# ScalarE reads MoE1's relu input from PSUM twice; VectorE subtracts in SBUF

## The chip, the cores and the metric

The kernel runs on one core of a Trainium2 chip. The core has five engines with a queue each: TensorE (PE; PEld is its weight load), VectorE (DVE), ScalarE (ACT), GpSimd (POOL) and SyncE (SP), which only issues DMAs here. Each queue is worked off in order, and engines wait for one another by semaphores. The metric is the time of one execution in microseconds on the device, the median of several runs.

## The reference

Three stages follow one another: chunked attention, a mixture of four experts with relu (MoE1), and a feed-forward layer with a clipped gate (MoE2). All results are fp32; the two weights of the last stage come as 64-bit floats.

```python
scores = scale * q_c @ k_c^T            # chunks of 64 rows, 4 x 8 heads x 576 x 64
attn   = softmax(scores);  x = attn @ v_c          # x: 2304 tokens x 512

p = domain_probs / (domain_probs.sum(-1) + 1e-9)   # MoE1: 4 experts, F = 1024
for e in range(4):
    h = np.maximum(x @ w1[e], 0.0)
    out += p[:, e:e+1] * (h @ w2[e])

h = x @ w_in                                       # MoE2: 512 -> 2048 -> 512
g = h * np.clip(h + 3.0, 0.0, 6.0) / 6.0
return g @ w_out
```

## The kernel before, in words

The large products run in `float32r`. To keep precision, each operand is held as two parts, a high part (the value cast to `float32r`) and a low part (the value minus its high part), and each product is three matmuls: high x high, high x low, low x high (`HL`).

The 2304 tokens are cut into six blocks of 256 or 512 (`sizes`), and two blocks make a set. For each of the three sets the kernel goes through 12 groups of 512 hidden columns, 8 of MoE1 and then 4 of MoE2, and in each group through the blocks of the set. One group of one block is four h slots and four y slots. An h slot (`h_slot`, matmuls L424) computes 128 hidden columns, transposed, into a PSUM bank `psH`; there are two such banks. A y slot (`y_slot`, matmuls L479) multiplies one of the four hidden tiles `gts[f]` with the second weight, into up to four banks `psY` that collect over the four y slots.

Between them stands the relu. In MoE1 ScalarE writes the high part of `gt` from `psH` (L445), and VectorE writes the low part (L446), reading `psH` once more and the high part from SBUF. In MoE2 the gate needs ScalarE's L454 and L461 and VectorE's L458 and L462; L462 is a subtraction whose two inputs both lie in SBUF. The finished `psY` are added into `acc` by VectorE (L503, L507).

The order of the work is written out by hand: each slot issues its matmuls, then the low parts that the slot before left (`late`), then the pieces that a planner assigned to this slot (`early`, `post`) by estimated times. These pieces are the attention of later blocks (`Item`; for instance L315 and L327 on VectorE, L319 on ScalarE, L335 on TensorE), the weights' split into high part (L141, ScalarE) and low part (L142, GpSimd), and in the first set the conversion of the MoE2 weights from 64-bit floats (`Convert`): L163 and L164 on ScalarE, L168, L169, L172, L179 and L183 on VectorE, L184 and L185 on GpSimd. SyncE loads the weights some slots ahead. VectorE adds the finished `psY` of a group in the next group's first two h slots (`TAKE`).

Of the kernel before, what the change touches and what calls it, by code (L numbers as in the profile page):

```python
# [10 lines left out]
F32 = mybir.dt.float32  # L11
F32R = mybir.dt.float32r
U32 = mybir.dt.uint32
AF = mybir.ActivationFunctionType
ALU = mybir.AluOpType
# [10 lines left out]
def raw(ap):  # L26

    return ap.bitcast(F32)
# [3 lines left out]
def fused_kernel(ctx: ExitStack, tc: tile.TileContext, q, k, v, probs, w1, w2, win, wout, out):  # L32
    nc = tc.nc
# [4 lines left out]
    P = 128  # L38
# [22 lines left out]
    sp = pool("sp", 1)  # L61
# [168 lines left out]
    def bank(tag, name="ps"):  # L230
        return pp.tile([P, 512], F32, tag=tag, name=name, bufs=BANKS[tag])
# [139 lines left out]
    late, spread, turns = deque(), deque(), deque()  # L371
# [15 lines left out]
    def slot(pe, now, pre, tail, early, post, take):  # L387


        for fn in pre:  # L390
            fn()
        pe()
        for fn in tail:
            fn()
        old = list(late)
        late.clear()
        for fn in old:
            fn()
        while turns:
            turn(*turns.popleft())  # L400
        for fn in early:
            fn()
        now()
        for _ in range(min(take, len(spread))):
            spread.popleft()()
        for fn in post:
            fn()
# [6 lines left out]
    def h_products(gi, view, f, ds):  # L414

        blk, c0, n = view
        cs = slice(c0, c0 + n)
        w = ws[gi, "h", f].rearrange("p a (d f) -> p a d f", d=KD)
        if (gi, view, f) not in begun:
            begun[gi, view, f] = bank("h", "psH")  # L420
        ps = begun[gi, view, f]
        for d in ds:
            for i, (a, b) in enumerate(HL):
                nc.tensor.matmul(  # L424
                    ps[:, :n], w[:, a, d, :], xt[blk][:, d, b, cs],
                    start=(d == 0 and i == 0), stop=(d == KD - 1 and i == len(HL) - 1),
                )

    def h_slot(gi, view, f, pre, tail, early, post):
        g = gi % NG  # L430
        blk, c0, n = view
        cs = slice(c0, c0 + n)
        done = range(NP // 2) if (gi, view, f) in begun else ()
        if not done:
            begun[gi, view, f] = bank("h", "psH")
        ps = begun[gi, view, f]

        def pe():
            h_products(gi, view, f, [d for d in range(KD) if d not in done])

        gt = sp.tile([P, 2, n], F32R, tag="gt", name="gt", bufs=4, padded_shape=[P, 2, 512])
        gts[f] = gt
        if g < G1:
            def now():
                nc.scalar.activation(gt[:, 0], ps[:, :n], AF.Relu)  # L445
                late.append(lambda: nc.vector.scalar_tensor_tensor(  # L446
                    out=gt[:, 1], in0=ps[:, :n], scalar=0.0, in1=raw(gt[:, 0]), op0=ALU.max, op1=ALU.subtract
                ))
        else:
            u = sp.tile([P, n], F32, tag="u", name="u", bufs=2, padded_shape=[P, 512])  # L450
            r = sp.tile([P, n], F32, tag="r", name="r", bufs=2, padded_shape=[P, 512])

            def now():
                nc.scalar.activation(r, ps[:, :n], AF.Relu, bias=three)  # L454
                late.append(mid)

            def mid():
                nc.vector.scalar_tensor_tensor(  # L458
                    out=u, in0=r, scalar=6.0, in1=ps[:, :n], op0=ALU.min, op1=ALU.mult
                )  # L460
                nc.scalar.mul(gt[:, 0], u, 1.0 / 6.0)  # L461
                late.append(lambda: nc.vector.scalar_tensor_tensor(  # L462
                    out=gt[:, 1], in0=u, scalar=1.0 / 6.0, in1=raw(gt[:, 0]), op0=ALU.mult, op1=ALU.subtract
                ))
        slot(pe, now, pre, tail, early, post, TAKE[f])

    def y_slot(gi, view, f, pre, tail, early, post):
# [283 lines left out]
```

## Time and profile before

| what | value |
|---|---|
| median of three runs | 1308.83 us (1307.6 to 1308.86) |
| the profiled execution, its span | 1307.79 us, 1306.0 us |
| TensorE matmul busy, mean granted clock | 1269.9 us (97%), 0.992 |
| VectorE, ScalarE, GpSimd busy | 601.6, 439.2, 474.7 us |
| L445, relu on ScalarE | 200 instructions, 95.8 us |
| L446, low part on VectorE | 200 instructions, 107.5 us |

A row of the profile names a line, an engine, an operation, what it writes and reads, and how often. "Idle before" is time in which the engine stood still in front of such an instruction, with the one that ended the wait behind the arrow. [...] Busy times are of one profiled execution; they overlap between engines and don't add up to the span.

### The profile page before, as it was taken

To read this page: it belongs to the slowest core of one execution; us is meant where nothing else is said; L and a number is where in the kernel's file an instruction comes from. 1 tells how busy PE (TensorE), PEld (TensorE's weight loads), DVE (VectorE), ACT (ScalarE), POOL (GpSimd) and SP (SyncE) were. 2 spreads that over 40 slices of the span, in tenths; PEclk is the share of its full clock that TensorE was granted. 3 is DMA by queue.
4 is the path that set the end of the run, shared out by engine and by line. 5 is a ranking of instruction groups with operands and counts; after the bars stand their busy time and mean duration, and the time that the engine had idled before them with its cause. 6 is when DMAs were issued, how large, how long until landed. Compare 5 with 4: busy or idle time off the path is not lost.

```text
span 1306.0 us, 19473 instructions
## 1 busy us (share of the span) xinstructions
PE 1269.9 (97%) x7534; PEld 1082.4 (83%) x7534; DVE 601.6 (46%) x990; ACT 439.2 (34%) x880; POOL 474.7 (36%) x359
## 2 busy tenths in 40 slices
PE   8998889889999999999999999999999999999998
PEld 7887777778888888888888888888888888888887
DVE  4547898796355542222233345653222222233443
ACT  4333434333354332222232235433222222234332
POOL 3325677676232233333323233223333333323330
PEclk9999899899999999999999999999999999999999
DMA  7516665553334232222332233423222222222211
GB/s 175 135 63 179 186 189 176 169 162 129 96 91 106 73 97 81 65 65 65 87 83 74 65 101 83 106 68 112 66 63 64 63 65 64 65 59 63 65 33 49
DMA packets 170733, 124.01 MB, mean 95 GB/s; under 512 B 67984, under 2 KB 141712, under 8 KB 170640
## 3 DMA queue, kind: packets, MB, share of 16 engines
q1 hardware_dynamic: 170640, 122.76, 33.0%
q8 instruction: 59, 0.97, 0.3%
q14 instruction: 34, 0.28, 0.1%
HBM read 109.61 MB, written 13.11 MB: 94 GB/s over the span
## 4 chain that ended last, share of the span: by engine, by line
PE 81%; DVE 13%; ACT 2%; DMA 1%; issue 1%; SPq 1%; POOL 1%; DVEq 0%; ACTq 0%; POOLq 0%
PE psH L424 39%; PE psY L479 38%; DVE cm L172 2%; DVE cm L169 2%; DVE cm L168 2%; PE psS L303 1%; DVE ce L179 1%; DVE acc L503 1%; DVE acc L507 1%; DVE gt L446 1%; DVE cm L183 1%; PE psX L346 1%; DVE e L327 1%; PE psT L378 1%; PE psP L335 1%
## 5 line engine op out<-in xcount | busy, mean ns | idle before, releaser
L142 POOL TENSOR_TENSOR ws<-wr,ws 128x512 fp32r<-128x512 f32 x288 | 384.1, 1346 | 758.0 <-ACT ws L141 732.2
L424 PE MATMUL psH<-x,ws 128*128 128x256 f32 (+1 forms) x3552 | 630.7, 335 | 24.6 <-DVE gt L446 23.0
L424 PEld LDWEIGHTS psH<-x,ws 128*128 128x128 f32 x3552 | 545.5, 191 | 99.1 <-DVE gt L446 27.9
L479 PE MATMUL psY<-ws,gt 128*128 128x512 f32 x2592 | 607.2, 391 | 0.0
L479 PEld LDWEIGHTS psY<-ws,gt 128*128 128x128 f32 x2592 | 482.0, 188 | 98.9
L445 ACT ACTIVATE gt<-psH 128x256 fp32r<-128x256 f32 (+1 forms) x200 | 95.8, 479 | 514.2 <-PE psH L424 514.0
L446 DVE SCALAR_TENSOR_TENSOR gt<-psH,gt 128x256 fp32r<-128x256 f32 (+1 forms) x200 | 107.5, 539 | 233.8 <-ACT gt L445 233.8
L141 ACT CAST ws<-wr 128x512 fp32r<-128x512 f32 x288 | 170.3, 615 | 3.8 <-DMA wr<-in_moe_w_dram 2.2
L503 DVE SCALAR_TENSOR_TENSOR acc<-psY,pn,acc 128x512 f32<-128x512 f32 x126 | 89.2, 746 | 168.1 <-PE psY L479 168.1
L454 ACT ACTIVATE r<-psH,three 128x256 f32<-128x256 f32 (+1 forms) x96 | 55.7, 581 | 159.6 <-PE psH L424 158.7
L458 DVE SCALAR_TENSOR_TENSOR u<-r,psH 128x256 f32<-128x256 f32 (+1 forms) x96 | 53.0, 552 | 94.4 <-ACT r L454 94.1
L462 DVE SCALAR_TENSOR_TENSOR gt<-u,gt 128x256 fp32r<-128x256 f32 (+1 forms) x96 | 70.9, 739 | 46.9 <-ACT gt L461 46.8
L461 ACT ACTIVATE gt<-u 128x256 fp32r<-128x256 f32 (+1 forms) x96 | 50.6, 528 | 48.1 <-DVE u L458 48.0
L184 POOL TENSOR_TENSOR w<-w,ce 128x512 f32<-128x512 f32 x32 | 47.7, 1492 | 31.1 <-DVE ce L179 19.6
L507 DVE TENSOR_TENSOR acc<-psY,acc 128x512 f32<-128x512 f32 x54 | 36.0, 687 | 44.8 <-PE psY L479 44.8
L185 POOL TENSOR_TENSOR ce<-w,cm 128x512 f32<-128x512 f32 x32 | 43.6, 1362 | 2.5
L172 DVE SCALAR_TENSOR_TENSOR cm<-w,cm 128x512 uint32<-128x512 uint32 x32 | 35.9, 1123 | 1.1
L169 DVE TENSOR_SCALAR cm<-cm 128x512 uint32<-128x512 uint32 x32 | 35.5, 1110 | 1.1
L168 DVE TENSOR_SCALAR cm<-cm 128x512 f32<-128x512 f32 x32 | 30.1, 940 | 6.2 <-ACT cm L163 6.1
L319 ACT ACTIVATE e<-e 128x512 f32<-128x512 f32 x18 | 11.4, 633 | 52.9 <-DVE e L315 52.9
L363 DVE TENSOR_TENSOR x<-psX,x 128x128 fp32r<-128x128 f32 (+1 forms) x56 | 15.8, 324 | 26.7 <-ACT x L362 25.2
L163 ACT ACTIVATE cm<-w 128x512 f32<-128x512 f32 x32 | 21.5, 673 | 11.6 <-POOL ce L185 11.6
(47 smaller groups left out, 349.9 us busy)
## 6 DMA issues: line engine op xcount, KB each, us to landing
wr<-in_moe_w_dram SPq DMA_DIRECT2D x192, 256.0 KB, 2.8
wr<-win SPq DMA_DIRECT2D x48, 256.0 KB, 2.9
wr<-wout SPq DMA_DIRECT2D x48, 256.0 KB, 2.7
w<-in_moe_w_in_dram SPq DMA_DIRECT2D x16, 512.0 KB, 5.2
w<-in_moe_w_out_dram SPq DMA_DIRECT2D x16, 512.0 KB, 5.2
out_dram<-acc SPq DMA_DIRECT2D x18, 256.0 KB, 2.1
win<-ce SPq DMA_DIRECT2D x16, 256.0 KB, 4.0
wout<-ce SPq DMA_DIRECT2D x16, 256.0 KB, 3.1
```

What stands on the lines that cost most here:

```text
L141: nc.scalar.copy(t[:, 0], self.t)
L142: (eng or nc.gpsimd).tensor_tensor(out=t[:, 1], in0=self.t, in1=raw(t[:, 0]), op=ALU.subtract)
L168: nc.vector.tensor_scalar(out=m, in0=m, scalar1=W_LEAST, scalar2=W_MOST, op0=ALU.max, op1=ALU.min)
L169: nc.vector.tensor_scalar(out=mu, in0=mu, scalar1=4, scalar2=1, op0=ALU.logical_shift_left, op1=ALU.logical_shift_right)
L172: nc.vector.scalar_tensor_tensor(out=mu, in0=self.t[:, :, 1], scalar=0x80000000, in1=mu, op0=ALU.bitwise_and, op1=ALU.bitwise_or)
L424: nc.tensor.matmul(ps[:, :n], w[:, a, d, :], xt[blk][:, d, b, cs], start=(d == 0 and i == 0), stop=(d == KD - 1 and i == len(HL) - 1),)
L445: nc.scalar.activation(gt[:, 0], ps[:, :n], AF.Relu)
L446: late.append(lambda: nc.vector.scalar_tensor_tensor(out=gt[:, 1], in0=ps[:, :n], scalar=0.0, in1=raw(gt[:, 0]), op0=ALU.max, op1=ALU.subtract
L454: nc.scalar.activation(r, ps[:, :n], AF.Relu, bias=three)
L462: late.append(lambda: nc.vector.scalar_tensor_tensor(out=gt[:, 1], in0=u, scalar=1.0 / 6.0, in1=raw(gt[:, 0]), op0=ALU.mult, op1=ALU.subtr ...
L479: nc.tensor.matmul(ps, gt[:, a, j * P:(j + 1) * P], w[:, b, :], start=f == 0 and i == 0, stop=f == GF - 1 and i == len(HL) - 1,)
L503: nc.vector.scalar_tensor_tensor(out=t, in0=ps, scalar=p, in1=t, op0=ALU.mult, op1=ALU.add)
```

## The change

For MoE1 ScalarE reads the bank twice: once into the high part, as before, and once more in full fp32 into a new tile `h32` in SBUF. VectorE then subtracts the high part from `h32`, and no longer reads PSUM for it. The tile takes its place in the buffers of MoE2's tiles `u` (even f) and `r` (odd f), two buffers each. The max with zero, which VectorE computed anew, is now in ScalarE's second relu. Nothing else is changed.

```diff
         if g < G1:
+            h32 = sp.tile([P, n], F32, tag="ur"[f % 2], name="h32", bufs=2, padded_shape=[P, 512])
+
             def now():
                 nc.scalar.activation(gt[:, 0], ps[:, :n], AF.Relu)
-                late.append(lambda: nc.vector.scalar_tensor_tensor(
-                    out=gt[:, 1], in0=ps[:, :n], scalar=0.0, in1=raw(gt[:, 0]), op0=ALU.max, op1=ALU.subtract
+                nc.scalar.activation(h32, ps[:, :n], AF.Relu)
+                late.append(lambda: nc.vector.tensor_tensor(
+                    out=gt[:, 1], in0=h32, in1=raw(gt[:, 0]), op=ALU.subtract
                 ))
```

## Rows read from the trace of the kernel before

**Rows 1.** The page, busy us (share of the span) xinstructions of each engine.

```profile
PE 1269.9 (97%) x7534; PEld 1082.4 (83%) x7534; DVE 601.6 (46%) x990; ACT 439.2 (34%) x880; POOL 474.7 (36%) x359
```

**Rows 2.** Table by stretches: us, busy of each engine, granted clock, DMA share, GB/s.

```profile
99.00:297.00 198.00, 176.62 (x963) 147.82 (x963) 170.48 (x242) 76.26 (x149) 134.48 (x95) 0.95 0.59 180
...
528.00:561.00 33.00, 33.00 (x170) 28.29 (x169) 8.68 (x15) 8.17 (x17) 10.34 (x8) 1.00 0.22 65
```

**Rows 3.** Waits from 99 to 297 us: who for whom, us in total, times, longest.

```profile
PE psH L424 <- DVE gt L446: 21.0, 11, 4.3
...
DVE gt L446 <- ACT gt L445: 13.3, 11, 2.2
ACT cm L163 <- POOL ce L185: 11.6, 5, 3.1
...
DVE cm L168 <- ACT cm L163: 5.7, 10, 1.3
```

**Rows 4.** Timeline of one stall: start us, us, engine line op [idle before].

```profile
231.40 0.41 DVE L446 SCALAR_TENSOR_TENSOR gt<-psH,gt 128x256 fp32r<-128x256 f32 x1
...
231.86 4.61 PE L424 MATMUL psH<-x,ws 128*128 128x256 f32 x24 [1.96 <-DVE gt L446]
...
236.31 5.62 PE L479 MATMUL psY<-ws,gt 128*128 128x512 f32 x24
```

**Rows 5.** Groups by form, 99 to 297 us: count | busy, mean ns | idle before.

```profile
L169 DVE TENSOR_SCALAR cm<-cm 128x512 uint32<-128x512 uint32 x29 | 32.2, 1112 | 1.0
...
L183 DVE TENSOR_SCALAR cm<-cm 128x512 uint32<-128x512 uint32 x29 | 13.4, 461 | 1.0
L446 DVE SCALAR_TENSOR_TENSOR gt<-psH,gt 128x512 fp32r<-128x512 f32 x19 | 12.8, 685 | 7.7 <-ACT gt L445 7.7
...
L446 DVE SCALAR_TENSOR_TENSOR gt<-psH,gt 128x256 fp32r<-128x256 f32 x22 | 9.2, 418 | 5.6 <-ACT gt L445 5.6
```

**Rows 6.** Timeline of VectorE, its idle times in front of L446 and L168.

```profile
101.13 0.42 DVE L446 SCALAR_TENSOR_TENSOR gt<-psH,gt 128x256 fp32r<-128x256 f32 x1 [1.01 <-ACT gt L445]
...
133.09 0.69 DVE L446 SCALAR_TENSOR_TENSOR gt<-psH,gt 128x512 fp32r<-128x512 f32 x1 [1.18 <-ACT gt L445]
134.16 1.07 DVE L168 TENSOR_SCALAR cm<-cm 128x512 f32<-128x512 f32 x1 [0.38 <-ACT cm L163]
...
155.67 0.42 DVE L446 SCALAR_TENSOR_TENSOR gt<-psH,gt 128x256 fp32r<-128x256 f32 x1 [1.85 <-ACT gt L445]
...
260.84 0.81 DVE L168 TENSOR_SCALAR cm<-cm 128x512 f32<-128x512 f32 x1 [0.39 <-ACT cm L163]
...
295.89 0.69 DVE L446 SCALAR_TENSOR_TENSOR gt<-psH,gt 128x512 fp32r<-128x512 f32 x1 [1.25 <-ACT gt L445]
```

**Rows 7.** Timeline of TensorE at the last stall of the stretch.

```profile
290.68 7.22 PE L424 MATMUL psH<-x,ws 128*128 128x512 f32 x24 [3.51 <-DVE gt L446]
297.74 2.43 PE L479 MATMUL psY<-ws,gt 128*128 128x512 f32 x10
```

**Rows 8.** Timeline around 1208 us: MoE2's subtraction in SBUF, beside GpSimd and alone.

```profile
1207.56 1.32 POOL L142 TENSOR_TENSOR ws<-wr,ws 128x512 fp32r<-128x512 f32 x1 [5.64 <-ACT ws L141]
...
1208.05 1.38 DVE L462 SCALAR_TENSOR_TENSOR gt<-u,gt 128x512 fp32r<-128x512 f32 x1 [1.32 <-ACT gt L461]
...
1210.72 0.69 DVE L462 SCALAR_TENSOR_TENSOR gt<-u,gt 128x512 fp32r<-128x512 f32 x1 [0.70 <-ACT gt L461]
```

**Rows 9.** Timeline of VectorE: two steps of a conversion without GpSimd beside them.

```profile
209.56 0.43 DVE L169 TENSOR_SCALAR cm<-cm 128x512 uint32<-128x512 uint32 x1
...
211.21 0.43 DVE L183 TENSOR_SCALAR cm<-cm 128x512 uint32<-128x512 uint32 x1
```

**Rows 10.** Groups by form, whole span: ScalarE's relu.

```profile
L445 ACT ACTIVATE gt<-psH 128x512 fp32r<-128x512 f32 x88 | 52.6, 598 | 255.5 <-PE psH L424 255.5
L445 ACT ACTIVATE gt<-psH 128x256 fp32r<-128x256 f32 x112 | 43.1, 385 | 258.6 <-PE psH L424 258.5
```

**Rows 11.** Waits of TensorE, whole span.

```profile
PE psP L335 <- DVE e L327: 3.6, 4, 1.7
```

## The prediction

> **What bounds the kernel now.** I read the page first, then the waits, the table by stretches, the groups of the one stretch that stood out, and the timeline of its stalls. TensorE is busy 97% of the span [rows 1]: a change to the two vector engines can only win back what TensorE waits for, or make it wait more. Over most of the span there is nothing to win: from 528 to 561 us TensorE works all 33.00 us at clock 1.00, with VectorE at 8.68 [rows 2]. The stretch from 99 to 297 us is different. There the `moe2` weights are converted from 64-bit floats (`Convert`, L163 to L188) beside the first block set, VectorE is busy 170.48 of 198 us, GpSimd 134.48, and TensorE only 176.62 at a granted clock of 0.95. So 198.0 - 176.6 = 21.4 us are lost there, and about 0.05 x 198 = 10 us more to the lower clock.
>
> What TensorE waits for there has one name: L446, 21.0 us in 11 waits [rows 3]. L446 is the second reader of the bank `psH`, and `psH` has two banks. The timeline of one stall shows how it works [rows 4]: the 256-column h slots 0 and 1 run, VectorE is deep in a conversion, L446 for slot 0 comes only at 231.40, slots 2 and 3 start 0.05 us after its end, and the y slots follow when those are done, at 236.31. The chain is conversion -> low part of slot 0 -> two h slots -> y. VectorE is what is late, and TensorE's two h slots are put behind it.
>
> **What the edit takes away.** L446 no longer reads PSUM; both readings are ScalarE's, back to back, so slots 2 and 3 no longer wait for VectorE. But VectorE's subtraction is still in front of something: y slot f reads both halves of `gts[f]` (L479). So the chain becomes conversion -> low part of slot 0 -> y slot 0, with slots 2 and 3 off it. The wait moves three slots further and does not go. As VectorE is busy 86% of the stretch, the length of the stretch after the change is VectorE's work plus what VectorE still idles; I sum it from VectorE's side.
>
> *Idle time of VectorE that goes.* VectorE idles in front of L446 for 7.7 + 5.6 = 13.3 us in the stretch, in 11 waits [rows 5]. Three of about 1.0 us, one of them shown, lie before the first conversion and stay: -3.1. One of 1.2 us ending at 133.09 comes from ScalarE being held by the attention's exponential, and stays. The other 9.0 us, seven waits, are VectorE, having caught up, waiting for h slots that had started late because of it, the first at 155.67 and the last at 295.89 [rows 6]; with TensorE three slots further ahead they go. Of the ten waits of L168 for ScalarE's L163 (5.7 us) [rows 3], five of 0.27 to 0.64 us, at 134.16 the first and at 260.84 the last, stand behind such a late relu and go as well: 2.1 us. Sum 11.1 us; bounds 0 (TensorE never gets ahead) and 19 (13.3 + 5.7, all of it).
>
> *The end of the stretch.* The last stall releases slots 2 and 3 at 290.68 and y starts at 297.74 [rows 7]. After the change y 0 can start where L446 for slot 0 ends, slots 2 and 3 lying before it: 7.1 us once, and not once for each stall, since at the earlier ones VectorE, not TensorE, sets when the next low part comes. Bounds 0 and 7.1.
>
> *What VectorE pays.* The subtraction now has two inputs in SBUF. Undisturbed it costs the same: L462, the operation of that kind here, takes 0.69 us at 512 columns [rows 8], L446 0.69 and 0.42 [rows 5]. Beside a GpSimd operation that also reads SBUF, L462 takes 1.38 us, and ends 0.55 us after GpSimd's does; L446, with one input in PSUM, keeps its 685 and 418 ns means even in this stretch. So 41 operations that were free of GpSimd become exposed to it. Two estimates of the price. First, the conversion's own steps, exposed in the same way: undisturbed L169 takes 0.43 and L183 0.43 us [rows 9], in the stretch 1112 and 461 ns on average [rows 5], the largest and the smallest excess of the five: 0.68 and 0.03 us. The mean of the two, 0.36 us, times 41 is 14.8. Second, chance: GpSimd is busy 134.48 / 198 = 68% with operations of 134.48 / 95 = 1.42 us, so an operation that starts at any time waits 0.68 x 0.71 = 0.48 us; times 41 is 19.7. I take the middle, 17. Bounds: 41 times the excess of L183, 1.3 us, and of L169, 28 us. Not less than zero, since nothing that L446 waits for now goes from this operation.
>
> [...]
>
> *What ScalarE pays.* 200 more readings. A second reading takes at most a whole L445, 598 or 385 ns [rows 10]: 52.6 + 43.1 = 95.7 us, ScalarE from 439 to 535 us of 1306 [rows 1]. It can't be below zero, since nothing of ScalarE's goes. Elsewhere it is hidden: an h slot of 12 matmuls lasts 2.8 us at 512 columns, as 24 take 5.62 us [rows 4], and ScalarE is busy 8.17 of 33 us in the steady stretch [rows 2]. In the conversion stretch it adds at most 19 x 0.598 + 22 x 0.385 = 19.8 us to 76.26 of 198. Queued behind the second reading are the weight casts (L141) and the conversion's first step (L163); GpSimd and VectorE wait for those. VectorE being the later one there, I cost it at nothing; if that cover goes, each of the ten L163 waits is longer by 0.3 to 0.6 us, up to 5 us. A bank also becomes free earlier than by two engines in turn (0.60 + 0.69 against 0.60 + 0.6), which in the steady stretches nobody waits for.
>
> *SBUF and queues.* The new tile lies in the buffers of `u` and `r`, idle in MoE1; it is reused four h slots later, after y slots that need the same subtraction, so no wait is added. No DMA moves.
>
> **Sum.** 11.1 + 7.1 - 17 = 1.2 us gained. The profiled execution took 1307.79 us (span 1306.0 and 1.8 around it), 1.0 us under the median 1308.83 of the runs; it would become 1306.6, and the median 1307.6, which I round to 1307.5. A change under 0.2% (2.6 us) can't be told from none, so this reads as no change. TensorE's 21.0 us on L446 go from the trace, and come back as waits for the low part at L479.
>
> **Rivals.**
> *The collisions are mostly paid already* (faster). The operation behind a subtraction is often a conversion step that waits for the same GpSimd operation anyway: what the one waits, the other no longer does. Then the price falls to about 7 us and the gain is 11.1 + 7.1 - 7 = 11.2: 1297.6. For it: a GpSimd operation can be waited for only once, and there are 95 of them. Against: by the timeline some twelve of the 41 stand in front of an operation that reads PSUM, such as L503, or of a transposition, which pays nothing today.
>
> *VectorE and GpSimd hold each other up at the SBUF* (slower). Place: VectorE between 99 and 297 us. If each subtraction pays what L169 pays, 28 us, the sum is 18.2 - 28 = -9.8: 1318.6. It decides from 18.2 / 41 = 0.44 us per subtraction on, and is seen as slower from (18.2 + 2.6) / 41 = 0.51. For it: conversion steps leave GpSimd with a queue, and the low parts come right behind them; in order on TensorE stand also attention products (L335) that wait for VectorE's L327, 3.6 us in four waits [rows 11], so TensorE can't run ahead everywhere. Against: GpSimd still idles 198.0 - 134.5 = 63.5 us of the stretch.
> [...]
>
> *ScalarE becomes the gate of the banks.* It sits up to 3.1 us behind L163, 11.6 us in five waits for GpSimd's L185 in the stretch [rows 3], and the relu behind it now alone frees the bank. Only what exceeds an h slot (2.8 us, half of it at 256 columns) reaches TensorE: at most some 4 us, 1311.5 where all of it adds to the forecast. Against: L445 sits behind TensorE, not behind L163, in most waits.
>
> **Numbers.** Forecast (within 2.6 us, price between 15.6 and 20.8): 0.38, own range 1306.2 to 1311.4. Faster, price under 15.6: 0.34. Slower: 0.28, of which 0.24 for the collisions and 0.04 for ScalarE. The range runs from a price of 7.5 us (1298) to one of 26.5 (1317).
>
> **What would show it.** Right: no wait of L424 on the low part; waits of L479 on VectorE between 99 and 297 us of about 20 us; the new subtraction at 0.42 and 0.69 us outside the stretch and about 0.4 us longer in it; VectorE's busy time in the stretch up by some 17 us and its idle time in front of the low part nearly gone; nothing after 330 us moved but in time. Wrong: TensorE's lost time in the stretch under 12 us, or the low part there no longer than before (faster); or a stretch longer than 198 us with GpSimd's operations longer too (slower).

## The result, and the profile after

The changed kernel took 1316.96 us (median of 4 runs), the kernel before 1308.21 us beside it: ratio 1.0067, 95% interval 1.0054 to 1.0080, 8.8 us slower. The forecast was no change (1307.5 us); the time lies 0.04 us inside the upper end of the range, far from the forecast and in the part of the range that the prediction gave to its slower rivals. The profiled execution took 1317.56 us, 9.8 us more than the 1307.79 of before. The ratios of all runs leave out one slow execution, of 3236.53 us, among the six of e11.

The page after shows busy time of each engine, and the group of the new subtraction. They answer to [rows 1]: VectorE is busy 33.7 us longer (a third of it outside the conversion; behind 330 us TensorE waits for VectorE 1.9 us, against 2.1 before), ScalarE 73.3 us, TensorE 2.2 us.

```profile
PE 1272.1 (97%) x7534; PEld 1079.8 (82%) x7534; DVE 635.3 (48%) x990; ACT 512.5 (39%) x1080; POOL 482.8 (37%) x359
...
L449 DVE TENSOR_TENSOR gt<-h,gt 128x256 fp32r<-128x256 f32 (+1 forms) x200 | 145.9, 733 | 233.9 <-ACT h L448 233.7
```

The table by stretches of the kernel after (us, busy of each engine, TensorE's granted clock with 1.00 for full speed, DMA share, GB/s) answers to [rows 2]; a row for 297 to 330 us is added.

```profile
99.00:297.00 198.00, 174.73 (x965) 143.19 (x964) 179.91 (x234) 89.50 (x188) 134.73 (x91) 0.96 0.56 170
297.00:330.00 33.00, 27.94 (x141) 22.35 (x139) 32.42 (x35) 14.05 (x29) 25.44 (x17) 1.00 0.49 160
...
528.00:561.00 33.00, 33.00 (x170) 28.33 (x169) 9.01 (x15) 11.22 (x25) 10.33 (x8) 1.00 0.22 64
```

The same view of the kernel before, for the added row:

```profile
297.00:330.00 33.00, 32.56 (x170) 27.69 (x170) 21.73 (x30) 11.39 (x23) 21.43 (x16) 1.00 0.30 98
```

The steady stretch is as it was: TensorE 33.00 of 33.00 us. The conversion stretch lost 23.3 us of TensorE in place of 21.4, and the 33 us behind it 5.1 in place of 0.4. VectorE, at 21.73 us there before, is now busy 32.42 of 33: the conversion is not done by 330 us.

The waits from 99 to 297 us (who for whom, us in total, times, longest) in the kernel after answer to [rows 3].

```profile
ACT cm L163 <- POOL ce L185: 33.2, 10, 6.2
...
PE psY L482 <- DVE gt L449: 11.1, 13, 1.5
...
PE psP L335 <- DVE e L327: 8.2, 2, 5.5
...
DVE gt L449 <- ACT h L448: 7.2, 6, 1.7
...
DVE cm L168 <- ACT cm L163: 3.9, 5, 1.3
...
PE psY L482 <- DVE acc L506: 3.3, 3, 1.5
```

The wait of `psH` for the low part is gone, as the edit wants it. In its place TensorE waits for VectorE at three other points, 11.1 + 8.2 + 3.3 = 22.6 us against 21.0.

What sets the end is the length of the conversion on VectorE. From the start of the first L163 to the end of the last L183 VectorE runs 262 instructions in both kernels. The table by stretches for just this stage, before and then after:

```profile
108.40:316.80 208.40, 186.57 (x1013) 156.05 (x1013) 185.22 (x262) 82.72 (x162) 147.20 (x104) 0.95 0.56 174
```

```profile
111.20:329.10 217.90, 189.57 (x1020) 153.87 (x1020) 207.66 (x262) 98.90 (x205) 156.65 (x105) 0.96 0.54 167
```

It is 9.5 us longer: VectorE's busy time (the third engine) rose by 207.66 - 185.22 = 22.4 us, and its idle time fell from 208.4 - 185.2 = 23.2 to 217.9 - 207.7 = 10.2 us, by 12.9. The groups by form of this stage (count | busy, mean ns of one | idle before) say which operations; they answer to [rows 5]. Before:

```profile
L172 DVE SCALAR_TENSOR_TENSOR cm<-w,cm 128x512 uint32<-128x512 uint32 x32 | 35.9, 1123 | 1.1
L169 DVE TENSOR_SCALAR cm<-cm 128x512 uint32<-128x512 uint32 x32 | 35.5, 1110 | 1.1
L168 DVE TENSOR_SCALAR cm<-cm 128x512 f32<-128x512 f32 x32 | 30.1, 940 | 6.2 <-ACT cm L163 6.1
...
L179 DVE TENSOR_SCALAR ce<-cm 128x512 uint32<-128x512 uint32 x32 | 18.7, 584 | 0.9
L183 DVE TENSOR_SCALAR cm<-cm 128x512 uint32<-128x512 uint32 x32 | 14.7, 458 | 1.1
L446 DVE SCALAR_TENSOR_TENSOR gt<-psH,gt 128x512 fp32r<-128x512 f32 x20 | 13.5, 685 | 9.7 <-ACT gt L445 9.7
L446 DVE SCALAR_TENSOR_TENSOR gt<-psH,gt 128x256 fp32r<-128x256 f32 x24 | 10.0, 417 | 3.6 <-ACT gt L445 3.6
```

After:

```profile
L168 DVE TENSOR_SCALAR cm<-cm 128x512 f32<-128x512 f32 x32 | 38.3, 1198 | 3.9 <-ACT cm L163 3.9
L172 DVE SCALAR_TENSOR_TENSOR cm<-w,cm 128x512 uint32<-128x512 uint32 x32 | 32.0, 1001 | 1.1
L449 DVE TENSOR_TENSOR gt<-h,gt 128x512 fp32r<-128x512 f32 x20 | 31.5, 1595 | 1.7 <-ACT h L448 1.7
L169 DVE TENSOR_SCALAR cm<-cm 128x512 uint32<-128x512 uint32 x32 | 28.5, 891 | 1.1
...
L449 DVE TENSOR_TENSOR gt<-h,gt 128x256 fp32r<-128x256 f32 x24 | 20.8, 869 | 1.4 <-ACT h L448 1.4
L179 DVE TENSOR_SCALAR ce<-cm 128x512 uint32<-128x512 uint32 x32 | 17.6, 549 | 0.9
L183 DVE TENSOR_SCALAR cm<-cm 128x512 uint32<-128x512 uint32 x32 | 13.7, 427 | 1.1
```

The 44 subtractions went from 13.5 + 10.0 = 23.5 us to 31.5 + 20.8 = 52.3, 28.8 more and 0.65 us each. The five conversion steps together fell from 134.9 to 130.1 us. (28.8 - 4.8 = 24.0; the busy time counts 22.4, mostly because the last subtraction begins as the stage ends.)

Why a subtraction pays more than half a microsecond is seen in the timeline of all engines (start us, us, engine line op, [idle before]) at one place, first of the kernel before, where the two operations are L446:

```profile
289.60 0.43 DVE L183 TENSOR_SCALAR cm<-cm 128x512 uint32<-128x512 uint32 x1
289.64 1.53 POOL L184 TENSOR_TENSOR w<-w,ce 128x512 f32<-128x512 f32 x1 [0.36 <-DVE ce L179]
289.94 1.28 DVE L446 SCALAR_TENSOR_TENSOR gt<-psH,gt 128x512 fp32r<-128x512 f32 x2
```

The same place of the kernel after:

```profile
298.59 1.42 DVE L179 TENSOR_SCALAR ce<-cm 128x512 uint32<-128x512 uint32 x1
...
300.04 0.43 DVE L183 TENSOR_SCALAR cm<-cm 128x512 uint32<-128x512 uint32 x1
300.08 1.55 POOL L184 TENSOR_TENSOR w<-w,ce 128x512 f32<-128x512 f32 x1 [0.36 <-DVE ce L179]
...
300.38 3.53 DVE L449 TENSOR_TENSOR gt<-h,gt 128x512 fp32r<-128x512 f32 x2
...
301.71 1.65 POOL L185 TENSOR_TENSOR ce<-w,cm 128x512 f32<-128x512 f32 x1
...
303.32 1.76 POOL L142 TENSOR_TENSOR ws<-wr,ws 128x512 fp32r<-128x512 f32 x1
```

VectorE's last conversion steps release GpSimd's L184, which L185 follows at once. Low parts stand in VectorE's queue right behind those steps, and so fall on the two: two subtractions, 0.69 us each where nothing is beside them (e10), take 3.53 us and end 0.55 us after L185.

Not every low part stands there. Of the 44 of the stage, 15 come directly behind L183 and pay 1.11 us each, 16.6 us together; 7 come directly behind another low part and pay 6.6; 14 behind L506 pay 5.7; 7 behind L172, and one behind L315, pay nothing. An example of those that pay nothing:

```profile
203.15 0.69 DVE L172 SCALAR_TENSOR_TENSOR cm<-w,cm 128x512 uint32<-128x512 uint32 x1
203.76 0.42 DVE L449 TENSOR_TENSOR gt<-h,gt 128x256 fp32r<-128x256 f32 x1
```

GpSimd is in an operation at the start of 29 of the 44, which is 66% and near the 68% of the prediction. But those 29 come early in it: 1.24 us of GpSimd's operation are left on average.

### The profile page after: what moved, and what is told of

Its sections match the earlier page's. It is cut to its first block, busy times and chain, and to the rows that moved or that the text cites. A ratio compares the mean times of both kernels' runs of the same rounds, so it can differ in the third digit from the quotient of the medians.

```text
span 1315.8 us, 19779 instructions
## 1 busy us (share of the span) xinstructions
PE 1272.1 (97%) x7534; PEld 1079.8 (82%) x7534; DVE 635.3 (48%) x990; ACT 512.5 (39%) x1080; POOL 482.8 (37%) x359
## 4 chain that ended last, share of the span: by engine, by line
PE 76%; DVE 17%; DMA 2%; ACT 2%; issue 1%; POOL 1%; SPq 0%; POOLq 0%; DVEq 0%; ACTq 0%
PE psY L482 37%; PE psH L424 36%; DVE gt L449 3%; DVE cm L168 2%; DVE cm L172 2%; DVE cm L169 2%; DVE acc L506 1%; PE psS L303 1%; DVE ce L179 1%; DMA w<-in_moe_w_in_dram 1%; DVE cm L183 1%; DVE acc L510 1%; DVE e L327 1%; POOL ws L142 1%; PE psX L346 1%
## 5 line engine op out<-in xcount | busy, mean ns | idle before, releaser
L142 POOL TENSOR_TENSOR ws<-wr,ws 128x512 fp32r<-128x512 f32 x288 | 386.1, 1353 | 740.0 <-ACT ws L141 729.2
L482 PE MATMUL psY<-ws,gt 128*128 128x512 f32 x2592 | 617.6, 394 | 20.1 <-DVE gt L449 15.2
L424 PE MATMUL psH<-x,ws 128*128 128x256 f32 (+1 forms) x3552 | 620.3, 332 | 2.2 <-DVE u L461 0.9
L424 PEld LDWEIGHTS psH<-x,ws 128*128 128x128 f32 x3552 | 539.7, 189 | 71.9 <-DVE u L461 3.3
L482 PEld LDWEIGHTS psY<-ws,gt 128*128 128x128 f32 x2592 | 483.7, 189 | 128.1 <-DVE gt L449 24.0
L449 DVE TENSOR_TENSOR gt<-h,gt 128x256 fp32r<-128x256 f32 (+1 forms) x200 | 145.9, 733 | 233.9 <-ACT h L448 233.7
L506 DVE SCALAR_TENSOR_TENSOR acc<-psY,pn,acc 128x512 f32<-128x512 f32 x126 | 89.3, 747 | 153.2 <-PE psY L482 153.2
L448 ACT ACTIVATE h<-psH 128x256 f32<-128x256 f32 (+1 forms) x200 | 94.7, 474 | 0.0
L184 POOL TENSOR_TENSOR w<-w,ce 128x512 f32<-128x512 f32 x32 | 48.8, 1525 | 50.9 <-DVE ce L179 43.3
L185 POOL TENSOR_TENSOR ce<-w,cm 128x512 f32<-128x512 f32 x32 | 48.2, 1507 | 2.5
L168 DVE TENSOR_SCALAR cm<-cm 128x512 f32<-128x512 f32 x32 | 38.3, 1198 | 3.9 <-ACT cm L163 3.9
L163 ACT ACTIVATE cm<-w 128x512 f32<-128x512 f32 x32 | 21.7, 679 | 37.8 <-POOL ce L185 37.8
L319 ACT ACTIVATE e<-e 128x512 f32<-128x512 f32 x18 | 11.4, 633 | 63.5 <-DVE e L315 63.5
L172 DVE SCALAR_TENSOR_TENSOR cm<-w,cm 128x512 uint32<-128x512 uint32 x32 | 32.0, 1001 | 1.1
L169 DVE TENSOR_SCALAR cm<-cm 128x512 uint32<-128x512 uint32 x32 | 28.5, 891 | 1.1
```

The costliest lines, as they stand in the source:

```text
L142: (eng or nc.gpsimd).tensor_tensor(out=t[:, 1], in0=self.t, in1=raw(t[:, 0]), op=ALU.subtract)
L168: nc.vector.tensor_scalar(out=m, in0=m, scalar1=W_LEAST, scalar2=W_MOST, op0=ALU.max, op1=ALU.min)
L172: nc.vector.scalar_tensor_tensor(out=mu, in0=self.t[:, :, 1], scalar=0x80000000, in1=mu, op0=ALU.bitwise_and, op1=ALU.bitwise_or)
L424: nc.tensor.matmul(ps[:, :n], w[:, a, d, :], xt[blk][:, d, b, cs], start=(d == 0 and i == 0), stop=(d == KD - 1 and i == len(HL) - 1),)
L448: nc.scalar.activation(h32, ps[:, :n], AF.Relu)
L449: late.append(lambda: nc.vector.tensor_tensor(out=gt[:, 1], in0=h32, in1=raw(gt[:, 0]), op=ALU.subtract))
```

## The experiments

All 14 runs in one table; each ratio is to the kernel before on the same chip. A loss or gain in us is the ratio's distance from 1 times the median of the kernel before on that chip, unless it is said to be by the medians. The median of e11 is that of five executions. The last column is the time in the profile from the first to the last L183 (in e6 and e7, which have none, L179): 204.3 us before, 213.8 after.

| run | median us | ratio (95% interval) | first to last L183 |
|---|---|---|---|
| e1_second_reading | 1315.97 | 1.0055 (1.0036 to 1.0074) | 205.2 |
| e2_only_in_conversion | 1318.97 | 1.0075 (1.0058 to 1.0091) | 214.1 |
| e3_only_elsewhere | 1307.60 | 0.9991 (0.9981 to 1.0002) | 204.1 |
| e4_before_no_pool | 1276.42 | 0.9769 (0.9749 to 0.9788) | 172.4 |
| e5_after_no_pool | 1280.86 | 0.9800 (0.9779 to 0.9821) | 174.8 |
| e6_before_four_steps | 1295.70 | 0.9913 (0.9894 to 0.9932) | 192.0 |
| e7_after_four_steps | 1300.96 | 0.9950 (0.9931 to 0.9968) | 197.1 |
| e8_scalar_from_sbuf | 1314.31 | 1.0047 (1.0031 to 1.0062) | 206.8 |
| e9_before_pool_silent | 1278.04 | 0.9776 (0.9763 to 0.9789) | 172.0 |
| e10_after_pool_silent | 1276.25 | 0.9760 (0.9746 to 0.9773) | 171.0 |
| e11_scalar_in_conversion | 1311.70 | 1.0040 (1.0024 to 1.0055) | 206.5 |
| e12_scalar_elsewhere | 1309.31 | 1.0014 (1.0003 to 1.0024) | 201.4 |
| e13_vector_part_alone | 1318.76 | 1.0073 (1.0060 to 1.0086) | 213.2 |
| e14_vector_part_in_conversion | 1317.35 | 1.0065 (1.0052 to 1.0078) | 213.4 |

**Where the loss lies.** The changed form only in groups 2 to 7 of the first block set, beside the conversion, and its complement.

```diff
-        if g < G1:
+        if g < G1 and 2 <= gi < G1:        # e3: if g < G1 and not 2 <= gi < G1
+            ...                            # the changed form
+        elif g < G1:
             ...                            # the form before
```

> The new form only in groups 2 to 7 of the first set, which run beside the conversion of the 64-bit weights (48 subtractions of 200); the old form elsewhere. Theory: all of the loss is made there, 1314 to 1318 us; the new subtraction takes about 0.8 us at 256 columns and 1.5 at 512, TensorE waits at the y products and at the attention's transpose. Rival (part of it comes from the start of the kernel, where the changed kernel's first conversion came 2.8 us later, or from the later sets): 1309 to 1312 us.

> The complement: the new form in groups 0 and 1 of the first set and in the two later sets, the old form beside the conversion. Theory: no difference, 1306 to 1310 us, 152 new subtractions with means near 0.55 us at 256 columns and 0.75 at 512. Rival (the start or the later sets lose time): 1311 to 1314 us.

Measured: 9.8 us lost with the form beside the conversion alone, nothing with the form everywhere else (1.2 us gained, with an interval from 2.5 gained to 0.3 lost). In the changed kernel from 330 us on the new subtraction takes 692 ns on average at 512 columns and 524 at 256, so some of the 256-column ones are longer than 0.42 us; these, ScalarE's doubled readings and the shared buffers cost nothing there, where GpSimd and VectorE have little to do (10.33 and 9.01 of 33 us from 528 to 561 us). The whole loss is made in a fifth of the span.

**ScalarE's second reading, first try.** The kernel before, in which ScalarE writes the full relu from PSUM into a tile that nobody reads.

```diff
                 nc.scalar.activation(gt[:, 0], ps[:, :n], AF.Relu)
+                nc.scalar.activation(h32, ps[:, :n], AF.Relu)
                 late.append(lambda: nc.vector.scalar_tensor_tensor(
```

> ScalarE reads each MoE1 bank a second time into the new SBUF tile, but nobody reads that tile: VectorE still subtracts from PSUM and still frees the bank. Theory (the price is VectorE's, which meets GpSimd at the SBUF between 99 and 300 us): ScalarE's 95 us are hidden, time 1306 to 1310 us, TensorE waits for the subtraction at L424 as before, some 21 us. Rival (ScalarE's second reading delays the weight casts and the conversion's first step): most of the 8.8 us appear here, 1313 to 1317 us.

Measured: 7.2 us slower, but this can't be read as the price of the second reading: it came out ahead of VectorE's reading, so that a bank was held by three readings in turn, which neither kernel does. In later block sets the 48 matmuls of a group at 256 columns took 6.07 us in place of 5.81. Inconclusive.

**ScalarE's operation without the bank.** The added operation reads the high part from SBUF; the bank and VectorE's reading are as before. Then beside the conversion only, and everywhere else only.

```diff
                 ))
+                nc.scalar.activation(h32, raw(gt[:, 0]), AF.Relu)   # e11: if 2 <= gi < G1, e12: if not
```

> A cleaner form of the first experiment. There the second reading of the bank came out in front of VectorE's, so that a bank was held by three readings in a row, which cost TensorE 0.25 us in each 256-column group also in the later sets. Here ScalarE's added operation reads the high part in SBUF, of the same size and number, and does not touch the bank. Theory (ScalarE's time is hidden): 1306 to 1310 us. Rival (ScalarE's added 95 us delay casts and the conversion's first step): 1311 to 1316 us.

> The kernel before, with ScalarE's added operation (a relu of the high part from SBUF into the spare tile, PSUM untouched, VectorE's subtraction as before, its result unused) only in groups 2 to 7 of the first block set, beside the conversion. Theory: ScalarE's added operation stands in front of the conversion's first step L163 there, VectorE's L168 waits longer for it, and most of the 5 to 7 us that the added operation cost in the whole kernel lie here: 1310 to 1314, stage from the first to the last L183 of 206 to 208 us in place of 204.4. Rival, the cost lies at the start of the kernel or after the conversion: 1307 to 1309, stage at 204.4 plus or minus 0.7.

> The complement of the run before: the kernel before with ScalarE's added operation from SBUF everywhere but in groups 2 to 7 of the first block set. Theory: hidden, 1306 to 1309, as the changed form was hidden there (1307.6). Rival, the cost lies at the start of the kernel or after the conversion: 1311 to 1314, with the first L163 3 to 4 us later than in the kernel before (108.4 us).

Measured: 6.1, 5.2 and 1.8 us lost. So a longer ScalarE queue is not free beside the conversion while VectorE reads the bank as before. The waits of VectorE from 95 to 330 us in e11 show where; the row stood at 6.1 us in 11 waits before.

```profile
DVE cm L168 <- ACT cm L163: 10.4, 12, 1.3
```

The added operation stands in front of L163, and VectorE waits 4.3 us longer for it. The profiled execution of e11, 1309.88 us, is the fastest of its five, and its stage is only 2.2 us longer than before, so the trace does not settle how the 5.2 us come about. The 1.8 us of e12 (interval 0.4 to 3.1) have no place in the trace that I could name.

**GpSimd taken away.** In both forms first the conversion's two GpSimd steps are left out, then also the low parts of the weights of groups 2 to 8, which ScalarE writes as copies of the high part.

```diff
-            nc.gpsimd.tensor_tensor(out=self.low, in0=self.low, in1=self.e, op=ALU.mult)
-            nc.gpsimd.tensor_tensor(out=self.e, in0=self.low, in1=m, op=ALU.add)
...
+            if 2 <= self.key[0] <= G1:                               # e9, e10 only
+                nc.scalar.copy(t, self.t.unsqueeze(1).to_broadcast([P, 2, 512]))
```

> The kernel before without the conversion's two GpSimd operations (L184, L185): the converted weight is left as the power of two, so MoE2's weights are not the reference's. GpSimd's work between 99 and 297 us falls from 134 to some 56 us. Theory (GpSimd and VectorE exclude each other at the SBUF): VectorE's conversion steps come near their undisturbed 2.4 us, 2.4 x 29 = 70 in place of 122 us, TensorE's 21 us of waits for the low part fall to under 8: 1283 to 1295 us. Rival (VectorE is late by the order of its queue alone): above 1300 us.

> The changed kernel without the same two GpSimd operations. Theory: with GpSimd mostly silent the new subtraction costs 0.45 and 0.75 us, and only the advantage is left, banks freed by ScalarE: equal to the kernel before without these operations or up to 6 us faster. Rival (the loss comes from moving the wait to the y products and to the attention's transposes on TensorE, whatever GpSimd does): still 5 to 9 us slower than the kernel before without these operations.

> The kernel before without the conversion's two GpSimd operations, and with ScalarE writing the weights' low parts of groups 2 to 8 too (as a copy of the weight, so those products are not the reference's): GpSimd does nothing beside the conversion. Theory: VectorE's conversion steps and subtractions are at their undisturbed times, TensorE loses under 3 us in the stretch, 1268 to 1278 us.

> The changed kernel with GpSimd silent in the same way. Theory (all of the loss is that VectorE and GpSimd exclude each other at the SBUF): the subtraction takes 0.42 and 0.69 us, and the time is that of the kernel before with GpSimd silent within 2 us, or less. Rival (what is left with the weight split alone, 4.4 us, has another cause, such as the start or ScalarE): still 3 to 5 us slower.

Measured: the kernel before is 30.2 us faster without the conversion's two steps, below what was expected of e4. With half of GpSimd's work gone the changed form is 4.4 us behind by the medians, with all of it gone 1.8 us ahead (the intervals of each pair overlap a little). The groups by form from 99 to 297 us give the subtraction in e5 and in e10:

```profile
L447 DVE TENSOR_TENSOR gt<-h,gt 128x512 fp32r<-128x512 f32 x21 | 19.2, 913 | 11.2 <-ACT h L446 11.2
...
L447 DVE TENSOR_TENSOR gt<-h,gt 128x256 fp32r<-128x256 f32 x27 | 12.9, 478 | 9.6 <-ACT h L446 9.6
```

```profile
L450 DVE TENSOR_TENSOR gt<-h,gt 128x512 fp32r<-128x512 f32 x21 | 14.5, 690 | 19.2 <-ACT h L449 19.2
L450 DVE TENSOR_TENSOR gt<-h,gt 128x256 fp32r<-128x256 f32 x28 | 11.8, 420 | 18.7 <-ACT h L449 18.7
```

A 512-column subtraction takes 1595 ns beside all of GpSimd's work, 913 beside half, 690 beside none, and the loss goes 8.8, 4.4, -1.8 us. ScalarE's readings are all there in e10 and cost nothing. So GpSimd's work is needed for the loss. The times alone do not say why, since without GpSimd VectorE is busy only 132.79 of the 198 us in e10 and TensorE 197.47: VectorE no longer sets the length of the stage, and a longer subtraction could hide there. That the subtraction itself falls to 690 ns is the direct sign. Whether VectorE's exposure to GpSimd is enough for the loss was left.

**VectorE's part alone.** The changed kernel without ScalarE's second relu: VectorE's operation keeps its place and two SBUF inputs, both the high part. e13 in the whole kernel, e14 beside the conversion only, with the form before elsewhere.

```diff
-                nc.scalar.activation(h32, ps[:, :n], AF.Relu)
                 late.append(lambda: nc.vector.tensor_tensor(
-                    out=gt[:, 1], in0=h32, in1=raw(gt[:, 0]), op=ALU.subtract
+                    out=gt[:, 1], in0=raw(gt[:, 0]), in1=raw(gt[:, 0]), op=ALU.max
```

> The changed kernel with ScalarE's second relu left out: VectorE's operation keeps its place and its two SBUF inputs, but takes the high part for both (a max, so the values of the low part are not the reference's). ScalarE's work is that of the kernel before. Theory, the loss is VectorE's exposure to GpSimd: 1314 to 1318, L168's and L163's waits as in the changed kernel. Rival, the loss is mostly ScalarE's second operation (which alone cost 5 us beside the conversion in the run before), and VectorE's exposure only takes back what the free banks give: 1306 to 1311. In between: both have a part.

> The same edit (VectorE's operation with two SBUF inputs, high part for both, no second relu) only in groups 2 to 7 of the first block set, beside the conversion; the kernel before elsewhere. Theory, the loss is VectorE's exposure: 1315 to 1319, as the changed form had there (1318.97), and the stage from the first to the last L183 near 214 us. Rival, mostly ScalarE's: 1306 to 1312, stage 203 to 208 us.

Measured: 9.6 and 8.5 us lost, as much as by the whole change (8.8, interval 7.1 to 10.5). The table by stretches of e13's conversion stage, beside the two rows shown of before and after:

```profile
113.00:330.20 217.20, 187.49 (x1022) 152.68 (x1022) 207.47 (x261) 82.98 (x162) 156.65 (x105) 0.98 0.54 168
```

VectorE is busy 207.47 us as after (207.66), ScalarE 82.98 as before (82.72). VectorE's two SBUF inputs make the whole loss, and ScalarE's second reading adds nothing that these runs can tell; the intervals of the change, e13 and e14 are each 3.4 us wide, so a part of 2 us would not show.

**A version that beats both.** With VectorE as the bound of the stage, work taken from VectorE must pay. ScalarE's L163 can scale by 2^16 in the operation that it does anyway (median 674 ns in e6 and in the kernel before), which makes the flip of an exponent bit in L179 and L183 needless: L183 goes, and L179 only masks. e7 is the same with the changed form.

```diff
-            nc.scalar.activation(self.m, ..., AF.Abs)
+            nc.scalar.activation(self.m, ..., AF.Abs, scale=2.0 ** 16)
-            ... scalar1=W_LEAST, scalar2=W_MOST, op0=ALU.max, op1=ALU.min)
+            ... scalar1=W_LEAST * 2.0 ** 16, scalar2=W_MOST * 2.0 ** 16, op0=ALU.max, op1=ALU.min)
...
-                out=self.e.bitcast(U32), in0=mu, scalar1=0x40000000, scalar2=0xFF800000,
-                op0=ALU.bitwise_xor, op1=ALU.bitwise_and,
+                out=self.e.bitcast(U32), in0=mu, scalar1=0xFF800000, scalar2=None, op0=ALU.bitwise_and
-            nc.vector.tensor_scalar(out=mu, in0=mu, scalar1=0x40000000, scalar2=None, op0=ALU.bitwise_xor)
```

> The kernel before with one VectorE operation less in each conversion: ScalarE's Abs scales by 2 to the 16, which is exact and flips the exponent bit as L183 did, the clamp's bounds are scaled with it, and L183 is left out. 32 operations of 0.46 us go, 13 us of VectorE's 170 in the stretch, and one exposure to GpSimd each. Theory (VectorE's work sets the length of the stretch): 4 to 13 us faster, 1295 to 1304 us. Rival (GpSimd or the order of the queues sets it): within 2 us of 1308.

> The changed kernel with the same four-step conversion. Theory: in the changed kernel VectorE is busy without a break from 132 to 330 us, so the 13 us come off in full: 9 to 14 us faster than the changed kernel, 1302 to 1308 us, still slower than the kernel before with four steps by 2 to 8 us. [...]

Measured: 1295.70 us, 0.9913 of the kernel before, 11.4 us gained where VectorE's 32 L183 had taken 14.7. The waits of TensorE from 99 to 297 us in e6:

```profile
PE psH L422 <- DVE gt L444: 13.6, 10, 3.1
```

The old wait is smaller and still there. With the changed form it is 1300.96, 5.3 us behind e6: the form loses here too, in a stage where VectorE has less to do.

## Why the prediction was wrong, step by step

The sum of the prediction beside what the two profiles give:

| step | forecast us | measured us |
|---|---|---|
| idle time of VectorE that goes | -11.1 | -12.9 |
| what VectorE pays | +17 | +22.4 |
| the end of the stretch | -7.1 | -1.2 |
| ScalarE | 0 | 0 |
| sum, to the first relu of MoE2 | -1.2 | +8.3 |
| start of the kernel, and after that relu | 0 | +2.8 and -1.3 |

8.3 + 2.8 - 1.3 = 9.8 is the difference of the profiled executions. The 2.8 at the start can't be put down to the edit: the first L163 starts at 111.2 and 111.0 us in e2 and e14 too, whose code there is the one before, and at 111.9 in e3, which loses nothing. It goes with TensorE's granted clock in the first 99 us, which was 1.00 in the profile of before and 0.98 in the one after (tables by stretches, before and then after):

```profile
0.00:99.00 99.00, 91.26 (x898) 81.28 (x899) 47.47 (x102) 37.74 (x89) 30.47 (x30) 1.00 0.49 125
```

```profile
0.00:99.00 99.00, 89.99 (x877) 79.96 (x878) 50.70 (x100) 41.63 (x107) 30.25 (x29) 0.98 0.47 116
```

Of ten profiles, the three with 1.00 through all of these 99 us (before, e4, e6) have the first L163 at 108.4 to 108.9 us, the seven with less in a part of them (after, e1, e2, e3, e5, e7, e8) at 109.7 to 112.7. Whether the edit has a part in that start stays open. The -1.3 is the edit's: from the first relu of MoE2 to the end it is 959.6 to 959.8 us in the six profiles with VectorE's new form in the later sets (after, e3, e5, e7, e10, e13), and 960.6 to 961.2 in the nine where VectorE still reads the bank there, with e1 (964.4) aside.

**Right:** the wait of `psH` for the low part goes and comes back at the y products (L482 for L449), though with 11.1 us in the stretch and 14.6 to 330 us in place of about 20; behind the conversion little moves (1.3 us); the new subtraction takes 0.69 and 0.42 us where GpSimd is idle (e10); VectorE's idle time goes nearly as counted from [rows 6].

**Failed, first: "I take the middle, 17".** A subtraction pays 0.65 us, not 0.41. In the second estimate the chance of 68% held (29 of 44). What failed is the 0.71 us, half a GpSimd operation, that it put as the wait of "an operation that starts at any time". The low parts do not start at any time. Those that meet GpSimd come early in its operation, with 1.24 us of it left, and pay 1.0 us on average; the 15 right behind L183, which start some 0.3 us after L184, pay 1.11 us each.

The trace of before had this order, as at 289.94 us, where two L446 follow L183 and L184 has just begun. Between 99 and 297 us, 24 of the 41 L446 start while GpSimd is in an operation, and what is then left of these operations adds up to 24.3 us. That count would have put the price above 20.8, from where on the prediction itself called the change slower. The mean of L169 and L183 in the first estimate has no such reason behind it. The rival that collisions are mostly paid is right in kind and small: the conversion steps got 4.8 us back of the 28.8.

The timeline at 300 us has two subtractions ending 0.55 us after a GpSimd operation that they lay beside, as one does in [rows 8]. The second estimate alone falls short too, 19.7 for 41 against 28.8 for 44, because it took half an operation as the wait.

**Failed, second: "7.1 us once".** The prediction let y 0 start where the low part of slot 0 ends, slots 2 and 3 lying before it, and stopped there. The timeline of TensorE at the last stalls of the kernel after answers to [rows 7]:

```profile
314.36 5.82 PE L424 MATMUL psH<-x,ws 128*128 128x256 f32 x48
321.73 0.73 PE L482 MATMUL psY<-ws,gt 128*128 128x512 f32 x2 [1.55 <-DVE acc L506]
322.72 1.66 PE L482 MATMUL psY<-ws,gt 128*128 128x512 f32 x6 [0.26 <-DVE gt L449]
325.43 1.65 PE L482 MATMUL psY<-ws,gt 128*128 128x512 f32 x6 [1.05 <-DVE gt L449]
328.40 1.65 PE L482 MATMUL psY<-ws,gt 128*128 128x512 f32 x6 [1.31 <-DVE gt L449]
330.64 1.19 PE L482 MATMUL psY<-ws,gt 128*128 128x512 f32 x4 [0.59 <-DVE gt L449]
```

All four h slots run in one piece, as foreseen. Then every y slot waits for its own low part, with conversion steps between these on VectorE. TensorE is held until the last low part, and the time from the last L183 to the first relu of MoE2 is 26.9 us in place of 28.1.

With 22.4 in place of 17, 1.2 in place of 7.1 and 12.9 in place of 11.1 the sum comes out at 8.3 lost.

**ScalarE "at nothing"** holds for this change: e13 and the changed kernel lose the same. Its cover was not VectorE's lateness as such. In the form before, an extra operation of ScalarE cost 5.2 us (e11). In the changed kernel L163 waits 33.2 us for GpSimd's L185 (11.6 in [rows 3]), L168 waits less for L163 than before, and the second relu fits into that wait. This fits the rows, but was not tried by itself.

**The slower rival** named the place and the mechanism, and 1318.6; it took 28 us as the price, with nothing back from the conversion steps (22.4 net), and kept the 7.1 (1.2). The two errors are 5.6 and 5.9 us and cancel, so that its time came within 2 us is luck in part. The prediction held the attention's L327 to be a small matter from [rows 11]: it now holds TensorE 8.2 us in the stretch, since what was a wait at `psH` turns up at whichever product needs VectorE next.

## What to carry to other kernels

Moving an operand of VectorE from PSUM into SBUF was no neutral move here beside a busy GpSimd (a 512-column low part went from 685 to 1595 ns): price such a move from the timeline, by what is left of GpSimd's operation wherever this operation starts (here 24.3 us over 41, where 28.8 over 44 were paid), and not with GpSimd's mean load and half an operation. The wait at one product did not go away, since later work on TensorE needed the same late engine (21.0 us at `psH` became 22.6 at three other points); with VectorE busy 86% of the stretch, what paid was to take work from it, as one of its 32-times-repeated steps folded into ScalarE did (11.4 us), or from the engine that holds it up: without GpSimd's two steps, which the result needs, the kernel before was 30 us faster (e4).

## What the runs showed of the hardware

- VectorE's 512-column low part with one of its two inputs in PSUM took 685 ns beside GpSimd's full load, with both in SBUF 1595 beside it and 690 without (e10). Two inputs in SBUF brought no gain: 690 against 685 ns.
- GpSimd pays too, and less: L185 took 1364 ns on average in the stage before and 1511 after, L142 1456 and 1512.
- One more ScalarE operation behind each relu, 0.42 us long at 256 columns and 0.63 at 512 (e8) and needed by nobody, cost 5.2 us beside the conversion (e11), in a stretch in which ScalarE is busy 76 of 198 us before. VectorE's wait for L163, in front of which it stands, grew by 4.3 us.
